# The output's DMA issued by ScalarE, and the first load of the q weights cut into two by partitions

## The chip, the core and the metric

The kernel runs on one core of one Trainium2 chip. The metric is the device time of one execution in microseconds (us); the time before is the median of three runs, 1303.96 us (1303.87 to 1304.36).

## What is computed

One decode step of attention over a long cache, beside a small gated MLP. Everything is 32-bit floating point.

```
# x: [2, 1, 512]; k_cache, v_cache: [2, 8, 32768, 128]; wq: [512, 4096]; wo: [4096, 512]
xn = layernorm(x)
q  = xn @ wq                                  # 32 heads of 128, four to one cache head
p  = softmax(q . k_cache * 128 ** -0.5)
s  = (p . v_cache) @ wo
h  = relu(xn @ w1 + b1) ** 2                  # w1: [512, 1792]
g  = silu(h @ w2 + b2)
out = x + s * g                               # [2, 1, 512]
```

The two caches are 512 MiB together; wq and wo are 8 MiB each, w1 and w2 3.5 MiB each.

## The kernel before, in words

The 16 pairs of cache head and batch are worked through one after another. Each pair has 32768 keys and as many values, each as two blocks of 8 MiB. A block goes to 128 partitions, 64 KiB in each. Two buffers hold them: `kring`, a ring of three half blocks of keys, and `vbuf`, one block of values. VectorE transposes keys (line 309), TensorE forms scores from them (line 270), ScalarE moves the scores and takes the exponential, TensorE applies the probabilities to the values (line 280).

**All big loads are issued by SyncE (SP), in one order, through the helper `load` (line 84).** That helper waits for the marks it is given, issues the DMA and counts on a semaphore, 16 for each DMA. What a mark says is when the buffer comes free: a key slot when VectorE has transposed it, `vbuf` when TensorE has read it. The order at the start is: wq into `vbuf` (line 138), the first key block, half of the second key block, then w1 into `vbuf`, which waits for the last matmul that reads wq (line 210), and so on. ScalarE issues four small loads of its own at the start: x, b1, b2, and x once more in the shape of the output.

wq lies in `vbuf` with row p of the buffer holding four rows of the matrix, 4 x 4096 numbers, so partition p receives one run of 64 KiB. TensorE's q projection waits for the count that `load` returned for wq, and for the normalised x; the chain for x runs on VectorE meanwhile.

**The end.** The last 8 MiB are wo, in seven loads that become smaller. When the last of them has landed, TensorE finishes the output projection (line 535), VectorE multiplies by the gate (line 572) and adds x (line 573), and then:

```
SP.wait(t)                   # t: the mark of line 573
last.after(sync.nop())
sync.dma_start(out2..., fin[0:P:Y, :]).then_inc(sent, 16)
sync.sem_clear(range(min(ids), max(ids) + 1))
sync.wait_ge(sent, 16)
sync.sem_clear(sent)
```

SP waits, issues the output (line 578: 8 partitions, 512 bytes in each), clears all counting semaphores while it is under way (line 580), waits for its landing and clears that semaphore too (line 582).

Of the kernel before, what the change touches and what calls it, by code (L numbers as in the profile page):

```python
# [11 lines left out]
P = 128  # L12
# [4 lines left out]
Y = 16  # L17
# [35 lines left out]
def gqa_decode_kernel(nc, x, kc, vc, wq, wo, w1, b1, w2, b2, out):  # L53
# [5 lines left out]
    ND = D // P  # L59
# [9 lines left out]
    out2 = out.rearrange("b s d -> (b s) d")  # L69

    def sb(name, *shape):
        return nc.alloc_sbuf_tensor(name, (P,) + shape, F32).ap()

    def bank(name, n=1):
# [3 lines left out]
    SP, ACT, DVE, POOL, TE = (Lane(nc, e, n) for e, n in (  # L78
        (nc.sync, "sp"), (nc.scalar, "act"), (nc.vector, "dve"), (nc.gpsimd, "pool"), (nc.tensor, "pe")))
    tensor, vector, scalar, gpsimd, sync = nc.tensor, nc.vector, nc.scalar, nc.gpsimd, nc.sync  # L80

    def load(lane, dst, src, sem, *marks):
        lane.wait(*marks)
        return sem.after(lane.eng.dma_start(dst, src))  # L84

    def dma(name):
        return Count(nc, name, 16)
# [39 lines left out]
    def load_k(m):  # L127
        a = m % 2
        return load(SP, kring[:, a * SLOT:(a + 2) * SLOT, :], k_rows(m), k_sems[a], transposed(max(2 * m - 2, -1)))

    vflat = vbuf.rearrange("p r d -> p (r d)")
    wq_t = vflat.rearrange("p (d f) -> p d f", d=ND)
# [2 lines left out]
    kflat = kring.rearrange("p r d -> p (r d)")  # L135
    wo_t = [kflat[:, a * SLOT * DH:a * SLOT * DH + 16 * D].rearrange("p (r e) -> p r e", r=16) for a in (2, 0)]

    wq_in = load(SP, wq_t, wq.rearrange("(p d) f -> p d f", p=P), dma("wq"))
    k0_in = load_k(0)
    load_k_half(1, 1)  # L140

# [9 lines left out]
    t = POOL(lambda: gpsimd.memset(ident, 0.0))  # L151
# [36 lines left out]
    t = DVE(lambda: vector.tensor_reduce(st[:, 0:1], xt, axis=AX.X, op=ALU.add), x_in)  # L188
    t = DVE(lambda: vector.tensor_scalar(st[:, 0:1], st[:, 0:1], 1.0 / D, None, op0=ALU.mult), t)
    t = DVE(lambda: vector.tensor_scalar(xn, xt, st[:, 0:1], None, op0=ALU.subtract), t)  # L190
    t = DVE(lambda: vector.tensor_mul(sq, xn, xn), t)
    t = DVE(lambda: vector.tensor_reduce(st[:, 1:2], sq, axis=AX.X, op=ALU.add), t)
    t = DVE(lambda: vector.tensor_scalar(st[:, 1:2], st[:, 1:2], 1.0 / D, 1e-5, op0=ALU.mult, op1=ALU.add), t)
    t = ACT(lambda: scalar.activation(st[:, 2:3], st[:, 1:2], AF.Sqrt), t)
    t = DVE(lambda: vector.reciprocal(st[:, 3:4], st[:, 2:3]), t)
    t = DVE(lambda: vector.tensor_scalar(xn, xn, st[:, 3:4], None, op0=ALU.mult), t)  # L196
    xnT = sb("xnT", ND, 32)
    TE.wait(t, have_ident)
    for d in range(ND):
        t = TE(lambda: tensor.transpose(mx_ps[:, d * P:(d + 1) * P], xn.rearrange("p (k d) -> p d k", d=ND)[:, d], ident))  # L200
# [5 lines left out]
    for f in range(2):  # L206
        for d in range(ND):
            for g in range(NG):
                cc = f * NG + g
                t = TE(lambda: tensor.matmul(pT_ps[32 * g:32 * g + 32, f, :], xnT[:, d, :],  # L210
                                             wq_t[:, d, cc * 512:(cc + 1) * 512], start=(d == 0), stop=(d == ND - 1)))
# [11 lines left out]
    for f in range(2):  # L223
        for h in range(REP):
            i = f * REP + h
            qr = kt[1].rearrange("p a b -> p (a b)")[:, i * 512:(i + 1) * 512].rearrange("p (e a w) -> p e a w", e=4, a=4)
            t = DVE(lambda: vector.tensor_copy(qr, pT_ps[:, f, h * DH:(h + 1) * DH].rearrange("p (e w) -> p e w", e=4)[:, :, None, :]  # L227
                                               .to_broadcast([P, 4, 4, 32])), q_done[f])
            t_ps = qbanks[i % 4]
            TE.wait(t, *(copied[i - 4:i - 3] if i >= 4 else ()))  # L230
            for e in range(4):
                t = TE(lambda: tensor.transpose(t_ps[:, e * P:(e + 1) * P], qr[:, e].rearrange("p a w -> p (a w)"), ident))
            v = t_ps.rearrange("p (e g y) -> p g e y", e=4, g=NG)
            for b in range(B):
                t = ACT(lambda: scalar.copy(qT[:, b, f * NG:(f + 1) * NG, h, :], v[:, :, :, Y * b]), t)
# [51 lines left out]
    def te_max(on):  # L287
        return on.after(tensor.transpose(mx_ps[:, 0:P], rm.to_broadcast([P, P]), ident))  # L288
# [25 lines left out]
    def dve_max(mark, on):  # L314
        return DVE(lambda: vector.tensor_tensor_reduce(scf[0], scf[0], scf[1], 1.0, -3.4e38, ALU.add, ALU.max, rm), mark, on=on)  # L315

    def dve_bias(mark, on):
        return DVE(lambda: vector.tensor_tensor_reduce(junk, mx_ps[:, 0:P], other, -SCALE, 3.4e38, ALU.add, ALU.min, nm), mark, on=on)  # L318
# [16 lines left out]
    def act_exp(mark, on):  # L335
        return ACT(lambda: scalar.activation(scf[0], scf[0], AF.Exp, bias=nm, scale=SCALE, accum_out=l), mark, on=on)  # L336
# [39 lines left out]
    for d in range(ND):  # L376
        for g in range(NG):
            t = TE(lambda: tensor.matmul(pj_ps[32 * g:32 * g + 32, :FG], xnT[:, d, :], w1_t[:, d, g * FG:(g + 1) * FG],  # L378
                                         start=False, stop=(d == ND - 1)))
    h1 = oflat[:, 0:FG]  # L380
    t = DVE(lambda: vector.tensor_scalar(h1, pj_ps[:, :FG], 0.0, None, op0=ALU.max), t)  # L381
    h2 = oflat[:, FG:2 * FG].rearrange("p (j w) -> p j w", j=FJ)
    hv = h1.rearrange("p (w j) -> p j w", j=FJ)
    t = DVE(lambda: vector.tensor_mul(h2, hv, hv), t)  # L384
# [6 lines left out]
    for j in range(FJ):  # L391
        g = j % NG
        t = TE(lambda: tensor.matmul(acc_ps[32 * g:32 * g + 32, :], hT[:, j, :], w2_t[:, j, :], start=(j < NG), stop=(j >= FJ - NG)))
# [13 lines left out]
    t = DVE(lambda: vector.tensor_copy(ysb, acc_ps), mlp_done)  # L407
# [9 lines left out]
    for j in range(4):  # L417
        t = TE(lambda: tensor.matmul(fin_ps[32 * j:32 * j + 32, 0:P], ones[0:1, 0:32], b2t[:, j * P:(j + 1) * P],
                                     start=False, stop=True, skip_group_check=True))
    t = ACT(lambda: scalar.activation(sg, fin_ps[:, 0:P], AF.Sigmoid), t)  # L420
# [4 lines left out]
    t = dve_max((EV.sem, 5), None)  # L425
    TE.wait(t)
    t = te_max(TE.sem)
    t = act_exp(dve_bias(t, None), None)
# [95 lines left out]
    def columns(r0, r1):  # L524
        TE.wait(wo_in[r0])
        for r in range(r0, r1):
            g = r % NG
            i = TE(lambda: tensor.matmul(pj_ps[32 * g:32 * g + 32, :], oR[:, r, :], wo_t[r // 16][:, r % 16, :], start=(r < NG), stop=(r >= 20 - NG)))
        return i

    def columns4(r0, r1):
        TE.wait(wo_in[r0])
        for r in range(r0, r1):
            for j in range(4):
                i = TE(lambda: tensor.matmul(acc_ps[32 * j:32 * j + 32, 0:P], oR[:, r, :], wo_t[r // 16][:, r % 16, j * P:(j + 1) * P],  # L535
                                             start=False, stop=(r == 31), skip_group_check=True))
        return i
# [8 lines left out]
    t = ACT(lambda: scalar.copy(o_sb, o_ps), PV.at(L + 3))  # L546
    TE.wait(kept, t)
    te_fin()
    hkv, b = divmod(NS - 1, B)
# [3 lines left out]
    t = DVE(lambda: vector.tensor_mul(om.rearrange("p b h a -> p (b h) a"), oT.rearrange("p b h -> p (b h)")[:, :, None].to_broadcast([P, B * HQ, 4]),  # L553
                                      blocks[:, None, :].to_broadcast([P, B * HQ, 4])), kept, have_o)
    TE.wait(t)
    for b in range(B):
        t = TE(lambda: tensor.matmul(mx_ps[:, 32 * b:32 * b + 32], om[:, b].rearrange("p h a -> p (h a)"), selg, start=True, stop=True))
    t = ACT(lambda: scalar.copy(oR.rearrange("p r y -> p y r")[:, 0:Y + 1:Y, :], mx_ps[:, 0:32 * B].rearrange("p (y r) -> p y r", y=B)), t, zero_oR)
    TE.wait(t)
    columns(0, 16)  # L560
    t = columns(16, 20)
# [8 lines left out]
    t = columns4(31, 32)  # L570
    fin = sb("fin", P)
    t = DVE(lambda: vector.tensor_mul(fin, gate, acc_ps[:, 0:P]), t)  # L572
    t = DVE(lambda: vector.tensor_add(fin, fin, x4), t)
    last = Count(nc, "last")
    SP.wait(t)
    last.after(sync.nop())
    sent = nc.alloc_semaphore("sent")
    sync.dma_start(out2.rearrange("b (j e) -> j b e", j=ND), fin[0:P:Y, :]).then_inc(sent, 16)
    ids = [s.num for s in Count.used]
    sync.sem_clear(range(min(ids), max(ids) + 1))  # L580
    sync.wait_ge(sent, 16)
# [24 lines left out]
```

## Time and profile before

| what | before |
|---|---|
| median of three runs | 1303.96 us |
| the profiled execution | 1303.92 us |
| its span, first to last instruction | 1302.6 us |
| mean granted TensorE clock | 0.78 |
| busy: PE, DVE, ACT | 48%, 48%, 10% |
| read from HBM | 561.01 MB, 431 GB/s over the span |

The span leaves out 1.3 us of the profiled execution's time, which lie around it. PE is TensorE, DVE is VectorE, ACT is ScalarE. Rows with SPq or ACTq are DMA issues on those engines' queues; they are not counted as busy. Line numbers in rows of before are those of the listing above. In the changed kernel all lines behind the first edit stand three lower in the file, and the output's issue is line 580.

### The profile page before, as it was taken

What the parts mean: (1) busy time and instruction counts of PE and PEld (TensorE: products, weight loads), DVE (VectorE), ACT (ScalarE), POOL (GpSimd) and SP (SyncE); (2) the same over time, 40 slices, a digit from 0 to 9 for tenths busy, and PEclk for the clock granted to TensorE, in tenths of its full rate; (3) what the DMA queues carried; (4) which work ended last, traced back from release to release, by engine and by line L of the source; (5) the groups of instructions that cost most, each with busy time, mean ns of one, the idle gap of its engine ahead of it and who ended that gap; (6) DMA issues with size and microseconds to landing.
All of it is one profiled execution on the core that took longest, in us unless ns stands there. A gap on an engine that the chain in (4) does not pass through costs nothing.

```text
span 1302.6 us, 10658 instructions
## 1 busy us (share of the span) xinstructions
PE 631.0 (48%) x4646; PEld 166.1 (13%) x4646; DVE 619.0 (48%) x305; ACT 128.7 (10%) x262; POOL 11.9 (1%) x41
## 2 busy tenths in 40 slices
PE   3455444445535445543545553454553445554465
PEld 1111110111101011110101111011110111111012
DVE  2565553436555344654435555343655534455410
ACT  0111011111001011000111101111100101101010
POOL 0000000000000000000000000000000000000000
PEclk9788777888767787777778767778867778877788
DMA  9999999999999999999999999999999999999998
GB/s 419 418 448 423 441 427 441 425 437 431 429 441 427 441 429 441 429 441 427 441 429 435 429 435 435 427 441 429 441 429 441 427 443 427 439 425 435 435 421 362
DMA packets 11135, 561.14 MB, mean 431 GB/s; under 512 B 1247, under 2 KB 1267, under 8 KB 1654
## 3 DMA queue, kind: packets, MB, share of 16 engines
q1 hardware_dynamic: 11100, 561.00, 99.6%
q8 instruction: 6, 0.10, 0.0%
q14 instruction: 3, 0.02, 0.0%
q10 hardware_dynamic: 26, 0.02, 0.0%
HBM read 561.01 MB, written 0.00 MB: 431 GB/s over the span
## 4 chain that ended last, share of the span: by engine, by line
DMA 75%; DVE 13%; issue 10%; PE 2%; SPq 0%; DVEq 0%
DMA kring<-in_A_k_cache 71%; DVE kt L309 12%; DMA kring<-in_A_v_cache 2%; DMA kring<-in_A_wo 2%; PE o_ps L280 1%; PE pj_ps L378 0%; PE ps_s L270 0%; SPq L84 0%; PE pj_ps L375 0%; DVE oR L384 0%; DVEq L308 0%; DVE hT L385 0%; DVE oR L381 0%; PE acc_ps L535 0%; DVE fin L572 0%
## 5 line engine op out<-in xcount | busy, mean ns | idle before, releaser
L309 DVE STREAM_TRANSPOSE kt<-kring 128x4096 f32<-128x4096 f32 x128 | 557.6, 4413 | 450.0 <-DMA kring<-in_A_k_cache 450.0
L270 PE MATMUL ps_s<-kt,qz 128*32 128x512 f32 x2048 | 333.1, 778 | 604.9 <-DVE kt L309 604.9
L280 PE MATMUL o_ps<-vbuf,pTh 128*16 128x512 f32 x1984 | 225.1, 606 | 6.2 <-DMA vbuf<-in_A_v_cache 4.5
L270 PEld LDWEIGHTS ps_s<-kt,qz 128*32 128x32 f32 x2048 | 67.8, 128 | 848.7 <-issue 675.0
L333 ACT ACTIVATE sc<-ps_s,halves 128x512 f32<-128x512 f32 x64 | 46.8, 730 | 870.0 <-PE ps_s L270 870.0
L280 PEld LDWEIGHTS o_ps<-vbuf,pTh 128*16 128x16 f32 x1984 | 56.9, 100 | 178.6 <-issue 155.9
L343 ACT COPY pTh<-pT_ps 64x256 f32<-64x256 f32 x128 | 46.9, 366 | 39.8 <-PE pT_ps L299 21.6
L315 DVE CUSTOM_DVE_ANT_0 sc<-sc 128x1024 f32<-128x1024 f32 x16 | 19.6, 1225 | 53.1 <-ACT sc L333 53.1
L318 DVE CUSTOM_DVE_ANT_0 junk<-mx_ps,other 128x128 f32<-128x128 f32 x16 | 4.7, 291 | 79.9 <-PE mx_ps L288 79.9
L336 ACT ACTIVATE sc<-sc,nm 128x1024 f32<-128x1024 f32 x16 | 18.4, 1149 | 106.7 <-DVE nm L318 106.7
L328 DVE TENSOR_REDUCE hr<-fin_ps 128x4 f32<-128x64 f32 x16 | 3.6, 225 | 46.5 <-PE fin_ps L292 46.5
L292 PE MATMUL fin_ps<-ident,o_sb 128*128 128x128 f32 x64 | 10.5, 286 | 18.0 <-DVE o_sb L485 17.2
L348 ACT COPY o_sb<-o_ps 128x512 f32<-128x512 f32 x15 | 8.8, 586 | 95.6 <-PE o_ps L280 95.6
L299 PE MATMUL pT_ps<-ident,sc 128*128 128x128 f32 x128 | 17.5, 282 | 0.0
L299 PEld LDWEIGHTS pT_ps<-ident,sc 128*128 128x128 f32 x128 | 15.3, 147 | 0.0
L280 PE MATMUL o_ps<-kring,pTh 128*16 128x512 f32 x64 | 9.6, 766 | 9.0 <-DMA kring<-in_A_v_cache 9.0
L493 POOL COPY oT<-ho 128x4 f32<-128x4 f32 x15 | 2.8, 188 | 1147.0 <-DVE ho L329 1147.0
L210 PE MATMUL pT_ps<-vbuf,xnT 128*32 128x512 f32 x64 | 8.8, 715 | 7.4 <-DMA vbuf<-in_A_wq 7.4
L227 DVE COPY kt<-pT_ps 128x512 f32<-128x512 f32 x8 | 5.0, 682 | 13.6 <-PE pT_ps L210 13.6
L485 DVE TENSOR_TENSOR o_sb<-o_sb,o_ps 128x512 f32<-128x512 f32 x15 | 10.2, 683 | 0.0
L292 PEld LDWEIGHTS fin_ps<-ident,o_sb 128*128 128x128 f32 x64 | 6.7, 140 | 21.8 <-DVE o_sb L485 20.1
L200 PE MATMUL mx_ps<-ident,kt 128*128 128x128 f32 x4 | 1.1, 435 | 14.3 <-DVE kt L196 14.3
(88 smaller groups left out, 102.8 us busy)
## 6 DMA issues: line engine op xcount, KB each, us to landing
kring<-in_A_k_cache SPq DMA_DIRECT2D x4, 4096.0 KB, 25.2
vbuf<-in_A_v_cache SPq DMA_DIRECT2D x2, 4096.0 KB, 26.6
vbuf<-in_B_w SPq DMA_DIRECT2D x2, 3584.0 KB, 29.2
kring<-in_A_wo SPq DMA_DIRECT2D x1, 4096.0 KB, 40.5
kring<-in_A_wo SPq DMA_DIRECT2D x3, 1024.0 KB, 24.1
kring<-in_A_wo SPq DMA_DIRECT2D x1, 512.0 KB, 26.9
kring<-in_A_wo SPq DMA_DIRECT2D x2, 256.0 KB, 27.1
kring<-in_A_k_cache SPq DMA_DIRECT2D x30, 29.8
```

Of the source, the lines that this page charges most:

```text
L210: t = TE(lambda: tensor.matmul(pT_ps[32 * g:32 * g + 32, f, :], xnT[:, d, :], wq_t[:, d, cc * 512:(cc + 1) * 512], start=(d == 0), stop=(d ...
L270: i = tensor.matmul(ps_s[32 * g:32 * g + 32, :], qz[:, 2 * y + e, :], kt[y][:, g * NO:(g + 1) * NO, 32 * e:32 * e + 32], start=(y == 0 and ...
L280: mm_ = tensor.matmul(o_ps[32 * g:32 * g + 16, :], pTh[:, 2 * g + c, 2 * i:2 * i + 2, :, :].rearrange("p o y h -> p (o y h)"), vt[:, lo:lo ...
L292: t = tensor.transpose(fin_ps[:, i * P:(i + 1) * P], o_sb[:, i * DH:(i + 1) * DH], ident)
L299: t = tensor.transpose(pT_ps[:, k // 4, (k % 4) * P:(k % 4 + 1) * P], p[:, k * P:(k + 1) * P], ident)
L309: KT[y].after(vector.transpose(kt[y], k_slot(q)[:, :, 64 * y:64 * y + 64]))
L315: return DVE(lambda: vector.tensor_tensor_reduce(scf[0], scf[0], scf[1], 1.0, -3.4e38, ALU.add, ALU.max, rm), mark, on=on)
L333: ACT(lambda: scalar.mul(sc[c][:, :, :, u], ps_s.rearrange("p (o w) -> p o w", w=32), halves[:, c:c + 1]), *marks, on=EV)
L336: return ACT(lambda: scalar.activation(scf[0], scf[0], AF.Exp, bias=nm, scale=SCALE, accum_out=l), mark, on=on)
L343: i = scalar.copy(pTh[64 * a:64 * a + 64, :, :, y, :], v[64 * y:64 * y + 64, :, :, a0, a, :])
L348: scalar.copy(o_sb, o_ps).then_inc(OE.sem, 32)
L485: DVE(lambda: vector.tensor_add(o_sb, o_sb, o_ps), on=OSR)
```

## The change

```
-    wq_in = load(SP, wq_t, wq.rearrange("(p d) f -> p d f", p=P), dma("wq"))
+    wq_p, wq_sem = wq.rearrange("(p d) f -> p d f", p=P), dma("wq")
+    load(SP, wq_t[0:16], wq_p[0:16], wq_sem)
+    wq_in = load(SP, wq_t[16:P], wq_p[16:P], wq_sem)
     k0_in = load_k(0)
...
-    SP.wait(t)
-    last.after(sync.nop())
     sent = nc.alloc_semaphore("sent")
-    sync.dma_start(out2.rearrange("b (j e) -> j b e", j=ND), fin[0:P:Y, :]).then_inc(sent, 16)
+    ACT.wait(t)
+    scalar.dma_start(out2.rearrange("b (j e) -> j b e", j=ND), fin[0:P:Y, :]).then_inc(sent, 16)
+    SP.wait(last.after(scalar.nop()))
     ids = [s.num for s in Count.used]
     sync.sem_clear(range(min(ids), max(ids) + 1))
```

wq arrives by two DMAs on one semaphore, 1 MiB to partitions 0 to 15 and 7 MiB to partitions 16 to 127, with 64 KiB in each partition as before; the projection waits for the count of both. The output is issued by ScalarE, whose wait for line 573 is part of the issuing instruction. A nop on ScalarE behind the issue lets SP go on, which then clears.

The head of SP's queue, both kernels in one piece; `vbuf<-in_A_wq` is the load of the q weights, the two rows behind it are the first keys:

```order
-L84 DMA vbuf<-in_A_wq 128x16384
+L84 DMA vbuf<-in_A_wq 16x16384
+L84 DMA vbuf<-in_A_wq 112x16384
 L84 DMA kring<-in_A_k_cache 128x16384
 L84 DMA kring<-in_A_k_cache 128x8192
```

One issue has become two, and the first keys stand one place further back.

The tail of SP's queue, with the last loads of wo; the rows named ISA are the two clears:

```order
 L84 DMA kring<-in_A_wo 128x1024
 L84 DMA kring<-in_A_wo 128x512 x2
-L578 DMA out<-fin 4x2x128 [waits dve]
-L580 ISA
-L582 ISA [waits sent]
+L583 ISA [waits last]
+L585 ISA [waits sent]
```

The output's issue has left SP, and its first clear now waits for the nop's count.

The tail of ScalarE's queue in the changed kernel, from the last probabilities (`pTh`) on; `o_sb` and `oR` are the last attention result on its way to the output projection:

```order
L346 COPY pTh<-pT_ps 64x64x4 [waits pv]
L346 COPY pTh<-pT_ps 64x64x4 x3
L549 COPY o_sb<-o_ps 128x512 [waits pv]
L561 COPY oR<-mx_ps 128x2x32 [waits pool,pe]
L580 DMA out<-fin 4x2x128 [waits dve]
```

The output's issue is ScalarE's last instruction in this list; before, the list ended with the copy to `oR`.

## The prediction

> **What bounds the kernel now.** I read the page first, its DMA part and its chain of waits, then busy time by windows, then the timeline of the first 45 us and of the last 20. Three lines of the page say what the end hangs on: SP's DMA queue, what was read in all, and the shares of the chain that ended last.
>
> ```profile
> q1 hardware_dynamic: 11100, 561.00, 99.6%
> ...
> HBM read 561.01 MB, written 0.00 MB: 431 GB/s over the span
> ...
> DMA 75%; DVE 13%; issue 10%; PE 2%; SPq 0%; DVEq 0%
> ```
>
> The 16 DMA engines are at work for 99.6% of the span for SP's queue alone, while TensorE and VectorE are busy for less than half. The windows (the last two columns are the engines' mean share and the rate) show that this holds from the start, and that there is no slack in between:
>
> ```profile
> 0.00:1.70 1.70, 0.00 (x0) 0.00 (x0) 0.68 (x2) 0.00 (x0) 0.93 (x8) 1.00 0.00 0
> ...
> 6.00:23.00 17.00, 1.26 (x8) 0.89 (x12) 3.80 (x9) 0.20 (x1) 0.00 (x0) 1.00 1.00 433
> 100.00:1200.00 1100.00, 526.28 (x3828) 133.41 (x3828) 544.94 (x242) 107.44 (x213) 8.66 (x28) 0.77 1.00 433
> ```
>
> Nothing moves in the first 1.7 us; from 6 us on the rate is 433 GB/s, the same as over 1100 us of the middle. So time that the DMA engines lose anywhere is lost at the end, and time that they win is won. Both edits are judged by that: the split changes when and how fast the first 8 MiB move, the other lies behind the last byte loaded.
>
> **The split of the first load.** The timeline of the start, with issue times and lengths, and the DMA view's row for this load (median us from issue to landing last):
>
> ```profile
> 0.74 0.39 SPq L84 DMA_DIRECT2D vbuf<-in_A_wq  x1
> 0.92 0.48 DVE L148 MEMSET kt<- 128x512 f32 x1 [0.92 <-PEq L595]
> 1.20 0.89 SPq L84 DMA_DIRECT2D kring<-in_A_k_cache  x2
> 1.43 1.22 ACTq L84 DMA_DIRECT2D kt<-in_A_x  x1
> 2.69 0.31 ACTq L84 DMA_DIRECT2D b1t<-in_B_b  x1
> 3.03 0.26 ACTq L84 DMA_DIRECT2D b2t<-in_B_b  x1
> 3.33 0.61 ACTq L84 DMA_DIRECT2D x<-in_A_x  x1
> ...
> 10.30 0.69 DVE L188 TENSOR_REDUCE st<-kt 128x1 f32<-128x512 f32 x1 [7.28 <-DMA kt<-in_A_x]
> ...
> 15.51 0.29 DVE L201 COPY xnT<-mx_ps 128x128 f32<-128x128 f32 x1 [1.22 <-PE mx_ps L200]
> ...
> 22.87 8.84 PE L210 MATMUL pT_ps<-vbuf,xnT 128*32 128x512 f32 x64 [7.39 <-DMA vbuf<-in_A_wq]
> ...
> 31.84 0.33 SPq L84 DMA_DIRECT2D vbuf<-in_B_w  x1
> ...
> 42.20 4.45 DVE L309 STREAM_TRANSPOSE kt<-kring 128x4096 f32<-128x4096 f32 x1 [7.87 <-DMA kring<-in_A_k_cache]
> ```
>
> ```profile
> vbuf<-in_A_wq SPq DMA_DIRECT2D x1, 22.0
> ```
>
> The load is 128 rows of 64 KiB, 8.39 MB. At 433 GB/s that is 19.4 us, so 2.6 of the 22.0 us are start-up, and an engine with 8 of the 128 rows needs 19.4 / 8 = 2.42 us for one.
>
> What it adds: a second issue, by the first one's row about 0.4 us of SP. The keys are issued that much later, at 1.6 instead of 1.20; the wq load is then under way for another 21 us (22.74 less 1.6), so this costs nothing. If that cover were gone it would cost 0.4.
>
> What it may win: one row per engine is set up sooner than eight. The pace of 433 reaches back from the landing at 22.74 to 3.3 us; first bytes move after 1.70. So at most 1.6 us lie there, part of it the landing itself, and at least nothing; nearest is the issue itself, which for the load of 4 rows took 0.31 us and for 128 rows 0.39. I take 0.2, closer to that.
>
> What it may cost: the first DMA fills 16 adjoining partitions and nothing else, with up to 16 engines at once. Every big load in this trace spans all 128, so no row shows how fast an eighth of the partitions can be filled. I bound it. At the quick end every engine keeps its pace: the first load takes one row, 2.4 us, the second seven rows, 17.0, together 19.4, and nothing is lost. At the slow end a partition takes no more than the full load gave it, 64 KiB in 19.4 us: then the first load takes 19.4 us for its 1 MiB, and the second, whose 112 partitions are limited in the same way, another 19.4. The sum is 38.8, a loss of 19.4. An overlap of the two on different engines lies between. No row is nearer to one end than to the other, so I take the middle, 9.7 us, and keep 0 and 19.4.
>
> [...]
>
> Does a late wq reach the end? PE's row shows that the projection waited 7.39 us for this load; xnT was ready at 15.80. The x load, which VectorE waited 7.28 us for, has 7 us of cover by the same row, and more as wq gets later. Behind wq stand the first keys and half of the next, 12.6 MB, 29 us of transfers, until about 51.9; w1, which waits for the projection, was issued at 31.84, so 20 us early. A wq that comes 9.7 us late moves both, the cover stays, and the engines never run dry. The delay passes to the end in full.
>
> **The output on ScalarE.** The end of the timeline, with ScalarE's last instruction, and from the list of SP's waits (us in total, times, longest) the one for the output:
>
> ```profile
> 1287.94 0.27 ACT L558 COPY oR<-mx_ps 128x64 f32<-128x64 f32 x1 [2.48 <-PE mx_ps L557]
> ...
> 1300.40 0.29 DVE L573 TENSOR_TENSOR fin<-fin,x 128x128 f32<-128x128 f32 x1
> 1300.82 0.68 SPq L578 DMA_DIRECT2D out<-fin  x1
> ```
>
> ```profile
> SPq L582 <- DMA out<-fin: 0.9, 1, 0.9
> ```
>
> VectorE is done at 1300.69; SP issues 0.13 us later and takes 0.68, until 1301.50; the span ends 1.1 us after that, of which SP waits 0.9 for the landing.
>
> With the wait inside the issue the step from VectorE is that of the x load at the start: its wait for line 148 ended at 1.40, the issue begins at 1.43, so 0.03 in place of 0.13, a gain of 0.1. The issue itself on ScalarE: the fourth of the rows at the start has the output's shape, 8 pieces of 512 bytes, and took 0.61, so 0.07 less than SP's 0.68. Its bounds are ScalarE's quickest, 0.26, and its first, 1.22, in case the engine needs that again after 1.3 ms without one. So the term is -0.17, between -0.52 and +0.44; I take -0.17, by the row of the same shape. Nothing is queued behind the waiting instruction on ScalarE but the nop, and ScalarE has been idle since 1288.21, so the wait holds up nobody. SP's clear moves from behind its own issue to behind ScalarE's nop. It starts perhaps 0.1 us later and has the 0.9 us of the landing to hide in; beyond 0.9 it would show in full.
>
> The sum: 1303.92, the profiled execution (its span and 1.3 around it; 0.04 below the median), -0.17 for the output, +9.7 for the split, in which the 0.2 of an earlier start is lost: 1313.5.
>
> **The rivals.** *Not slower: the engines, not the place, set the pace.* 433 GB/s over 16 engines is 27 GB/s for each, and if that is an engine's own limit, 16 rows in 16 adjoining partitions move as fast as any. For it: while 433 was measured from 6 to 23 us, the four small loads of 1 to 8 partitions were landing beside the stream, and the rate was no lower than later. Against it: those are a few KB, far too little to show a limit. It gives 1303.92 - 0.17 - 0.2 = 1303.6, from 1302 with all of the start-up's 1.6 won to 1304.4 with a first issue of 1.22. It decides if the first load's rows stay below twice their 2.42 us; up to there the loss is under 2.4.
>
> *Dearer: the second load is dealt in the same way.* If its 112 rows are handed out so that the 16 engines again write 16 adjoining partitions at a time, there are eight such steps rather than one. At the middle price of 10.9 us for the first (between 2.4 and 19.4) eight take 87, 68 more than now: 1372. For it speaks only that nothing shows how rows are dealt; against it, that a full load, dealt so, would not reach 433.
>
> *The change does not do what it says:* the engines start no earlier, since the first bytes wait for something other than the setting up of rows. Without a limit by place that leaves the output's -0.17, 1303.8, and belongs to the first rival.
>
> **How the numbers follow.** 0.2% is 2.6 us, about what a measurement of this kernel can tell from no change. Nothing in the sum can win that: 1.6 and 0.5 are the ceilings, and both would have to be met; 0.02 for faster. If the time of a row in the first load is 1, 2, 4 or 8 times 2.42 us, the first two are within 2.6 us of now and the last two are not, which is even; that sixteen streams into one eighth of the memory should find no narrower way than into all of it seems the less likely of the two, so 0.55 for the forecast, 0.05 for the dearer case, 0.38 for the first rival. That makes slower 0.60. The forecast's own range is 1306.5 to 1323.2, the slow end. As the first rival has more than 0.2, the range reaches down to it: 1303.0 to 1323.2. It leaves out the dearer case, the rival's lowest tail and nothing else: cut anywhere above 1313.5 it would hold less than 8 in 10 only if the slow end is as likely as the middle, and no row says that it is not.
>
> **What would show it.** Right: the matmuls of line 210 (213 in the new file) start near 32.5 instead of 22.87, the rate of the first 20 us is well under 433, SP's issue of w1 follows near 41.5, the first transposition of keys near 52, and from there on every row of before stands some 9.7 us later, with the last wo load included; the output's issue on ScalarE begins 0.03 us behind VectorE and lasts 0.6. Wrong: the projection starts at 22.9 or a little before, and the rate from 6 to 23 us is 433 as now; then the first rival holds. A start beyond 43 would be the dearer case, and an output issue of 1.2 us would upset the second term.

## The result, and the profile after

The changed kernel takes 1325.62 us, the median of six runs (1323.73 to 1325.79), beside 1304.16 for the kernel before in the same session (1303.87 to 1305.26): a ratio of 1.016, 95% interval 1.015 to 1.017. It is slower by some 21.5 us. Slower was forecast, with 1313.5; the time lies 2.4 us above the upper end of the range, 1323.2.

The page of the changed kernel shows where to look. Its row of GB/s has 40 slices of 33 us each:

```profile
span 1324.4 us, 10659 instructions
...
GB/s 218 350 434 444 424 434 437 428 437 437 428 435 435 435 430 433 437 428 435 437 428 433 439 426 437 437 428 435 435 435 430 433 437 428 435 437 428 433 427 345
...
q1 hardware_dynamic: 11104, 560.99, 99.6%
```

The first two slices are at 218 and 350; from the third on the rate is that of before. The share of SP's queue is still 99.6%, and the DMA row of the page shows 9 tenths or more in every slice but the last, at 218 GB/s as at 434: here the share doesn't tell a fast stream from a jammed one. The rate does.

The start of the changed kernel's timeline, with the two issues of wq in its first row:

```profile
0.74 0.85 SPq L84 DMA_DIRECT2D vbuf<-in_A_wq  x2
...
21.78 0.69 DVE L191 TENSOR_REDUCE st<-kt 128x1 f32<-128x512 f32 x1 [18.77 <-DMA kt<-in_A_x]
...
26.99 0.29 DVE L204 COPY xnT<-mx_ps 128x128 f32<-128x128 f32 x1 [1.22 <-PE mx_ps L203]
...
44.94 8.79 PE L213 MATMUL pT_ps<-vbuf,xnT 128*32 128x512 f32 x64 [17.98 <-DMA vbuf<-in_A_wq]
...
53.87 0.33 SPq L84 DMA_DIRECT2D vbuf<-in_B_w  x1
...
64.25 17.42 DVE L312 STREAM_TRANSPOSE kt<-kring 128x4096 f32<-128x4096 f32 x4 [7.89 <-DMA kring<-in_A_k_cache]
```

The projection starts at 44.94, 22.07 us later than before; w1 is issued 22.0 later, the keys are transposed 22.05 later, and the span is 21.8 longer. One delay, taken on before 45 us, is carried to the end. x came 11.5 us later as well, at 21.78, but xnT was ready 17.7 us before the projection could use it.

Windows split that delay into its two loads. They count a packet's bytes and its time at its start, and a packet is one 64 KiB row here. So the rate times the length of a window says how many rows began in it, and the share, times that length and 16 engines, how long these rows took in all:

```profile
1.70:2.70 1.00, 0.00 (x0) 0.00 (x0) 1.00 (x5) 0.00 (x0) 0.28 (x2) 1.00 8.56 1049
2.70:10.00 7.30, 0.00 (x0) 0.00 (x0) 0.32 (x3) 1.28 (x1) 0.00 (x0) 1.00 0.00 0
10.00:11.40 1.40, 0.00 (x0) 0.00 (x0) 0.00 (x0) 0.00 (x0) 0.00 (x0) 1.00 3.86 749
11.40:46.00 34.60, 2.19 (x12) 1.18 (x16) 3.80 (x9) 0.20 (x1) 0.00 (x0) 1.00 0.90 239
100.00:1200.00 1100.00, 529.33 (x3890) 136.29 (x3882) 542.11 (x249) 113.06 (x221) 10.00 (x30) 0.78 1.00 434
```

Between 1.7 and 2.7 us 1.05 MB begin, the 16 rows of the first load. Then for 7.3 us no row begins; the next 16 start between 10.0 and 11.4. So a row of the first load took about 8.5 us in place of 2.42; the share of 8.56 in the first window says the same, 8.56 us for each of its 16 rows. The second load follows, and the projection starts at 44.94: some 34 us for 7.3 MB, twice the 17.0 of full pace. The same first window of the kernel before:

```profile
1.70:2.70 1.00, 0.00 (x0) 0.00 (x0) 1.00 (x5) 0.00 (x0) 0.28 (x2) 1.00 2.96 1049
```

There too 16 rows begin, in the same microsecond. The smaller first portion did not start the engines sooner, as far as these windows show. By the share of 2.96 these first rows took 2.96 us each, a little more than the later 2.42.

The end of the changed kernel, its last two rows on VectorE and ScalarE's issue, with the waits of SP:

```profile
1322.31 0.29 DVE L576 TENSOR_TENSOR fin<-fin,x 128x128 f32<-128x128 f32 x1
1322.63 0.63 ACTq L580 DMA_DIRECT2D out<-fin  x1
```

```profile
SPq L583 <- ACTq L581: 30.7, 1, 30.7
...
SPq L585 <- DMA out<-fin: 0.9, 1, 0.9
```

The issue begins 0.03 us behind VectorE and takes 0.63; SP still waits 0.9 us for the landing, so its clear stayed hidden. From VectorE's end to the end of the span it is 1.8 us, 1.9 before.

### The profile page after: what moved, and what is told of

It reads as the page before. It is cut to its first block, busy times and chain, and to the rows that moved or that the text cites. A ratio compares the mean times of both kernels' runs of the same rounds, so it can differ in the third digit from the quotient of the medians.

```text
span 1324.4 us, 10659 instructions
## 1 busy us (share of the span) xinstructions
PE 626.4 (47%) x4646; PEld 165.7 (13%) x4646; DVE 618.9 (47%) x305; ACT 128.6 (10%) x262; POOL 11.9 (1%) x41
## 3 DMA queue, kind: packets, MB, share of 16 engines
q1 hardware_dynamic: 11104, 560.99, 99.6%
## 4 chain that ended last, share of the span: by engine, by line
DMA 74%; DVE 13%; issue 10%; PE 2%; another core or an unknown queue 1%; SPq 0%; DVEq 0%
DMA kring<-in_A_k_cache 67%; DVE kt L312 12%; DMA vbuf<-in_A_wq 3%; DMA kring<-in_A_v_cache 2%; DMA kring<-in_A_wo 2%; PE pT_ps L213 1%; PE o_ps L283 1%; PE pj_ps L381 0%; PE ps_s L273 0%; DVE kt L230 0%; SPq L84 0%; PE pj_ps L378 0%; DVE oR L387 0%; DVEq L311 0%
```

## The experiments

The theory after the result is an assumption, made from the first load's rows, which took 8.5 us each where 2.42 was the pace: partitions share ways into the memory that holds them, a way takes no more than one engine's pace, and a load is as slow as its engines crowd on ways. No trace shows a way; the runs show rates, and can fit the theory or not. Rivals: the rows read from HBM, the large memory, lie too close together (16 adjoining rows are 1 MiB in one place); two loads, or their semaphore, cost the time; ScalarE's issue does. Except for the first, all kernels are the kernel before, output issue included, with wq loaded differently; of their edits the new lines are shown.

**The output's edit alone.**

```
     wq_in = load(SP, wq_t, wq.rearrange("(p d) f -> p d f", p=P), dma("wq"))
...
-    SP.wait(t)
-    last.after(sync.nop())
...
-    sync.dma_start(...).then_inc(sent, 16)
+    ACT.wait(t)
+    scalar.dma_start(...).then_inc(sent, 16)
+    SP.wait(last.after(scalar.nop()))
```

> The kernel before with the output's edit alone: wq is one load again. The theory that the split carries the whole loss expects 1303.8, that is 0.1 to 0.2 us less than before, since in the changed kernel the issue began 0.03 us behind VectorE and took 0.63 us. The rival, that ScalarE's issue or the later clear has a part in the loss, expects more than 1306.

Measured: 1303.77 us (median of 11) beside 1304.0, ratio 0.9999, interval 0.999 to 1.0008. Its end:

```profile
1300.14 0.29 DVE L573 TENSOR_TENSOR fin<-fin,x 128x128 f32<-128x128 f32 x1
1300.47 0.63 ACTq L577 DMA_DIRECT2D out<-fin  x1
```

The span ends at 1302.2, 1.8 us after VectorE, as in the changed kernel. The edit has no part in the loss; its gain of 0.1 us in the profile is too small to be told from no change in the times.

**The split alone.**

```
+    load(SP, wq_t[0:16], wq_p[0:16], wq_sem)
+    wq_in = load(SP, wq_t[16:P], wq_p[16:P], wq_sem)
```

> The kernel before with wq in two loads, of partitions 0 to 15 and 16 to 127, and the output as before. If the split carries the whole loss, 1325.7 us, and the first matmul of the q projection starts near 44.9 us as in the changed kernel. If the two edits share the loss, clearly less.

Measured: 1325.52 us, ratio 1.0167 (1.0151 to 1.0182); the projection starts at 44.70. The split carries the whole loss.

**Two loads, cut along the rows.**

```
+    load(SP, wq_t[:, 0:1], wq_p[:, 0:1], wq_sem)
+    wq_in = load(SP, wq_t[:, 1:ND], wq_p[:, 1:ND], wq_sem)
```

> wq in two loads again, but cut along the rows: the first brings 16 KiB to each of the 128 partitions, the second 48 KiB. Both theories that lay the loss to what the first 16 rows have in common (adjoining partitions written, or adjoining memory read) expect about 1304, within 0.5 us of before. The rival that two loads on the queue, or their shared semaphore, cost the time expects 1320 or more.

Measured: 1303.91 us (median of 10), ratio 0.9999 (0.999 to 1.0008). Two loads cost nothing as long as each spans all partitions, and their shared semaphore costs nothing. Nor does a first portion of a quarter win anything.

**Place written or memory read.** Four kernels with eight loads of 16 partitions: adjoining or every eighth partition, from adjoining rows or from every eighth row.

```
+    for r in range(8):
+        wq_in = load(SP, wq_t[DST], wq_p[SRC], wq_sem)
# adj_adj:       DST 16 * r:16 * r + 16   SRC 16 * r:16 * r + 16
# adj_spread:    DST 16 * r:16 * r + 16   SRC r:P:8
# spread_adj:    DST r:P:8                SRC 16 * r:16 * r + 16
# spread_spread: DST r:P:8                SRC r:P:8
```

> wq in eight loads of 16 adjoining partitions each, from 16 adjoining 64 KiB rows each; the result is the reference's. Both theories, the place written and the memory read, expect eight times the first load of the changed kernel, some 9 us each, 72 in place of 19.4: 1357. If only the first load on the queue is slow (a start-up effect), 1304 + 7 = 1311.

> Eight loads of 16 adjoining partitions, but each from every eighth 64 KiB row of wq, so that the rows read lie 512 KiB apart; the rows go to other partitions than they should, so q is another one. The place theory expects the loss of eight slow loads, 1357. The theory of the memory read expects about 1304.

> Eight loads, each to every eighth partition, from 16 adjoining 64 KiB rows; q is another one here too. The place theory expects clearly less loss than with adjoining partitions: if ways are shared by groups of four and by partitions 32 apart, every eighth partition reaches eight ways, 4.84 us for each load, 38.7 in all: 1323. The theory of the memory read expects 1357.

> Eight loads, each to every eighth partition from every eighth row; the result is the reference's. The place theory expects 1323 as with adjoining rows, the theory of the memory read 1304. If both matter, the four kernels of this kind all differ.

| partitions written | rows read: adjoining | rows read: every eighth |
|---|---|---|
| adjoining | 1360.16 us | 1359.15 us |
| every eighth | 1325.59 us | 1325.27 us |

One run each, beside 1303.97 for the kernel before. Down a column the time changes by 34 us, along a row by about 1. Which rows are read makes no difference that single runs can tell. The windows over these loads, first adjoining to adjoining, then adjoining from every eighth row:

```profile
4.00:76.00 72.00, 1.13 (x4) 0.73 (x4) 3.80 (x9) 1.46 (x2) 0.00 (x0) 1.00 0.92 105
```

```profile
4.00:76.00 72.00, 1.13 (x4) 0.73 (x4) 3.80 (x9) 1.46 (x2) 0.00 (x0) 1.00 0.93 107
```

and the two kernels with every eighth partition, from adjoining and from spread rows:

```profile
4.00:42.00 38.00, 1.13 (x4) 0.73 (x4) 3.80 (x9) 1.49 (x2) 0.00 (x0) 1.00 0.94 194
```

```profile
4.00:42.00 38.00, 1.13 (x4) 0.73 (x4) 3.80 (x9) 1.49 (x2) 0.00 (x0) 1.00 0.94 195
```

Sixteen adjoining partitions take 105 to 107 GB/s, about four engines' worth of 27; every eighth takes 194, something over seven. The start-up rival, 1311, falls too: the rate is as low over all eight loads.

**Two loads of 64, four of 32 adjoining partitions.**

```
+    for r in range(0, P, W):          # W = 64 (halves), 32 (quarters)
+        wq_in = load(SP, wq_t[r:r + W], wq_p[r:r + W], wq_sem)
```

> wq in two loads of 64 partitions each. Theory of the place: ways into the memory are shared by adjoining partitions; in the changed kernel 16 of them took 1 MiB in about 9 us, four times 2.42. If the rate goes on doubling with the number of adjoining partitions, 64 reach the full rate and the time is 1304. If partitions 32 apart share a way, 64 reach half the rate, 4 MiB take 19.4 us, the two loads 38.8, and the time is 1323. The per-partition limit of the prediction gives half the rate as well. The rival that the memory read is the limit expects little loss, below 1310, since 64 rows lie as far apart as those of the full load's first steps.

> wq in four loads of 32 adjoining partitions. If a way belongs to four adjoining partitions and the four that lie 32 further, 32 adjoining partitions reach eight ways, as many as 64 do, and the time is 1326, that of the two loads of 64. If the rate goes with the number of adjoining partitions, 32 get half of what 64 get, four loads take 77 us, and the time is 1363.

Measured: halves 1326.57 us beside 1304.0, quarters 1324.89 beside 1305.01, one run each. The windows over the loads, halves first:

```profile
4.00:42.00 38.00, 1.13 (x4) 0.73 (x4) 3.80 (x9) 1.49 (x2) 0.00 (x0) 1.00 0.94 194
```

```profile
4.00:42.00 38.00, 1.13 (x4) 0.73 (x4) 3.80 (x9) 1.46 (x2) 0.00 (x0) 1.00 0.94 194
```

Both at 194: 64 adjoining partitions are no quicker than 32. That refutes a rate in proportion to their number, and the prediction's per-partition limit with it: that would have given 32 partitions a quarter of 433, 108 GB/s. It fits ways shared by partitions 32 apart. An estimate from the rates, at 27 GB/s for a way (433 over 16 engines): 105 is 3.9 ways for 16 adjoining partitions, so about four partitions to a way, and 194 is 7.2, which is nearer to eight than to four and is reached by 32 as by 64, so the second 32 add no ways. The expectations go further, with four adjoining partitions and the four that lie 32 further on one way. That is the author's assumption: the rates of these loads fit it, and no run shows which partitions share a way.

**Even, then odd partitions.**

```
+    for r in range(2):
+        wq_in = load(SP, wq_t[r:P:2], wq_p[r:P:2], wq_sem)
```

> wq in two loads of 64 partitions each, the even and the odd ones, so that each load has partitions in every part of the memory. The theory that it counts which ways the partitions of a load reach expects the full pace, 1304. The theory that it counts which way each engine writes at a time, with the rows dealt to the engines in runs of four, expects two engines on one way in each step (partitions 32 apart share one), 5.1 us for a row as in the two loads of 64 adjoining partitions, and 1326.

Measured: 1304.23 us, beside 1305.01 for the kernel before. The window and the start of the projection:

```profile
4.00:22.00 18.00, 1.13 (x4) 0.73 (x4) 3.80 (x9) 1.49 (x2) 0.00 (x0) 1.00 0.94 409
```

```profile
23.22 9.61 PE L212 MATMUL pT_ps<-vbuf,xnT 128*32 128x512 f32 x64 [7.35 <-DMA vbuf<-in_A_wq]
```

These 64 partitions, in every part of the memory, are at full pace. Some 112 rows begin in the window, so by its share a row took 2.4 us, as in a full load; the rate reads 409 in this window and 460 from 10 to 20 us, and the projection starts 0.35 us later than the 22.87 of before. The theory that 64 rows are dealt in runs of four expected 1326 and fell: in these loads of 16, 32 and 64 partitions the place of the partitions set the rate, 105 to 107 GB/s for 16 adjoining, 194 or 195 for 32 or 64 adjoining and for every eighth, full pace for every second.

**The large load first.**

```
+    load(SP, wq_t[0:112], wq_p[0:112], wq_sem)
+    wq_in = load(SP, wq_t[112:P], wq_p[112:P], wq_sem)
```

> wq in two loads as in the change, but the large one first: partitions 0 to 111, then 112 to 127. Theory of the dealing: a load of 112 rows is slow by itself, since engines meet on ways; it takes 24 us if they only meet where two runs of seven cross, and up to 34 as in the changed kernel, and the small one 9 behind it, so 1318 to 1328. The rival, that the large load is slow only because the first one left the engines jammed, expects 19.4 us or less for it and 9 for the small one: 1311 to 1313.

Measured: 1325.52 us beside 1305.01, as with the small one first. The window over the large load:

```profile
4.00:32.00 28.00, 1.13 (x4) 0.73 (x4) 3.79 (x9) 1.49 (x2) 0.00 (x0) 1.00 1.06 242
```

So 112 partitions are slow by themselves, at a good half of the full pace, though they lie in every part of the memory; no earlier load had jammed the engines. So it does not suffice that a load reaches every part.

**96 and 32 partitions.**

```
+    load(SP, wq_t[0:96], wq_p[0:96], wq_sem)
+    wq_in = load(SP, wq_t[96:P], wq_p[96:P], wq_sem)
```

> wq in two loads, of partitions 0 to 95 and 96 to 127. Theory of the dealing in runs: 96 rows go to the 16 engines in runs of six; counted by ways (four adjoining partitions and the four 32 further), two engines meet on two or three ways in each of the six steps, and as in the load of 112 every step then takes about 4.8 us for all, 28.8; the 32 rows behind it take 10.2 as in the four loads of 32; together 39 in place of 19.4, 1323.6. The rival, that only the fullest way counts, gives the large load eight rows of 2.42 on one way, 19.4, and 10.2 for the small one: 1314.

Measured: 1325.81 us beside 1303.93; the first window is at half pace:

```profile
4.00:32.00 28.00, 1.13 (x4) 0.73 (x4) 3.80 (x9) 1.48 (x2) 0.00 (x0) 1.00 1.03 216
```

The rival that only the fullest way counts expected 1314 and falls. Dealing in runs (each engine gets neighbouring rows, six of 96 or seven of 112), with every engine held up where two meet, is the author's estimate, from the 4.8 us of a row in the load of 112; it came within 2.2 us.

The traces hold a closer sign of runs, which no run was made to test. The sign holds only under the assumption of the expectations on which partitions share a way. Put four adjoining partitions and the four that lie 32 further on one way, and let each engine go through its run of seven in steps of one row. For partitions 16 to 127, engines would then meet on one way alone in the third and fourth step and on two in all others; for 0 to 111, on one in the fourth and fifth. The windows over the start of the third step in the changed kernel's second load, and over the rows behind it:

```profile
20.50:21.50 1.00, 0.00 (x0) 0.00 (x0) 0.00 (x0) 0.00 (x0) 0.00 (x0) 1.00 3.22 1049
23.50:24.50 1.00, 0.00 (x0) 0.00 (x0) 0.97 (x2) 0.00 (x0) 0.00 (x0) 1.00 3.29 922
25.00:26.00 1.00, 0.17 (x1) 0.18 (x2) 0.65 (x2) 0.05 (x1) 0.00 (x0) 1.00 0.47 131
```

and over the fourth step of the large load that comes first, and the rows behind it:

```profile
15.40:17.00 1.60, 0.00 (x0) 0.00 (x0) 0.07 (x1) 0.00 (x0) 0.00 (x0) 1.00 2.11 655
18.80:19.80 1.00, 0.00 (x0) 0.00 (x0) 0.94 (x2) 0.00 (x0) 0.00 (x0) 1.00 3.25 922
20.50:21.50 1.00, 0.53 (x3) 0.53 (x4) 0.41 (x1) 0.00 (x0) 0.00 (x0) 1.00 0.48 132
```

In each, sixteen rows begin in the first window, so all engines take part; fourteen rows follow about 3 us later and two only after 4.8. In the step before, a row took 4.8 to 4.9 us in both loads: in the changed kernel 16 rows begin from 15.5 to 17.0 us, with a share of 3.24 at 704 GB/s; in the other load the window from 10 to 20 us has 1.15 at 303 GB/s, which leaves 16 such rows beside the thirty listed. So the first quicker step is the third in one load and the fourth in the other, with two engines held back in it: where runs of seven put it, if the assumption holds.

## Why the prediction was wrong

- **What bounds the kernel, and that a loss at the start reaches the end:** right. 22.07 us at the projection, 21.8 at the end of the span.
- **The second issue hidden:** right; the keys were issued at 1.64 rather than 1.20, and two loads by columns cost nothing.
- **The start-up gain, 0.2 us:** nothing was won. 16 rows began between 1.7 and 2.7 us before and after.
- **The first load, between 2.4 and 19.4 us, middle 10.9:** about 8.5 by the windows, a loss of 6 where the term had 8.5 (5.6, against the 2.96 that the first rows took before). The mechanism was the one named, adjoining partitions; the slow end was too slow, since it counted by partition, which the loads of 32 partitions refute.
- **The second load, 17.0 to 19.4 us:** this is the step that failed. The bound said that 112 partitions are "limited in the same way", by what each took in the full load, and so can't need more than 19.4. They needed 34. What a partition took in the full load was carried over to a load of 112; no row showed that it holds there, and a load of 112 by itself runs at 242 GB/s. The term was 18.2 and measured 34, 16 us too little, of which the first load gave back 2.4. With the right size the sum would have been 1303.92 - 0.17 + (8.5 + 34 - 19.4) = 1326.9, near the 1325.62 measured.
- **The dearer rival** had the right question, how the rows of the second load are dealt, with too high a price (1372) and too low a chance. A case between, a row at twice its 2.42 us in the second load, was missing, and the range left it out.
- **The rival of no loss** falls with the four kernels of eight loads: 16 rows at a time ran at 105 to 107 GB/s into adjoining partitions and at 194 or 195 into every eighth, so an engine's pace is not all that counts, the place is. Its evidence, that a few KB beside the stream did not slow it, was as weak as stated.
- **The output on ScalarE:** step 0.03 us and issue 0.63, against 0.03 and 0.61; the gain in the profile was 0.1 rather than 0.17, since the issue took 0.02 us longer than put down and the landing some 0.03 longer than before.

What stays open is the rule by which rows are dealt to the engines. That 112 and 96 partitions run at about half pace (242 and 216 GB/s) and 64 alternate ones at full pace (2.4 us a row) is shown; that the former are dealt in runs is argued, from one time that came near and from where the quicker steps lie, and both rest on the assumption on which partitions share a way. Runs can't be the rule for every count: under the same assumption, runs of eight would put two engines on each way in use all through a full load, at half pace, and it has 433. Why two such meetings would hold up all sixteen engines, and not only those that meet, is not shown either.

## What to carry to other kernels

In this kernel the load of wq was best left spanning all 128 partitions, at 433 GB/s; lying in every part of them was enough for 64 alternate ones (1304.23 us), but not for 112 (242 GB/s) or 96 (216). A large load is better cut along its rows, where two pieces cost nothing (1303.91 beside 1304.0), than into blocks of adjoining partitions, where an eighth of it and the rest took some twice as long (8.5 + 34 us in place of 19.4). A bound on a piece that the trace has never shown must not borrow a figure of the whole, such as the 19.4 us in which each partition got its 64 KiB. And when the DMA engines are busy all the time, read GB/s beside their share: in the changed kernel the share is 0.90 at 239 GB/s and 1.00 at 434.

## What was not expected of the hardware

- 112 or 96 of 128 partitions are little faster than 64 adjoining ones: 242 and 216 GB/s against 194, where all 128 run at 433 and 64 alternate ones took 2.4 us a row, like a full load.
- While the big queue was jammed, a small load on another came later: x, 4 KB issued by ScalarE at 1.43 us in both kernels, was read by VectorE at 21.78 us instead of 10.30.
- Sixteen rows begin between 1.7 and 2.7 us (1049 GB/s in that window) whether the load has eight rows for each engine or one.
